# A fused attention and feed-forward kernel on one core: its head recut by deadline, later operands put in order two pairs ahead

**Chip, cores, metric.** One core of one Trainium2 chip. The time is device microseconds of one execution, in float32 input and output; lower is better. Executions of one kernel mostly agree within one or two per cent. A run more than 1.5% above the fastest of its kernel is classed "slow" and left out of every ratio here; the medians and ranges in the tables are of all runs.

## The reference

Eight batches, eight heads, 576 tokens and 16 "beacon" tokens of 64 columns. Attention with a causal mask (beacons are always seen), then two matrix products with a leaky ReLU between them. Cut to what matters:

```python
k_all = concatenate([beacon_k, k], axis=2); v_all = concatenate([beacon_v, v], axis=2)
scores = matmul(q, k_all^T) / sqrt(64)           # [8, 8, 576, 592]
scores = where(causal, -1e9, scores)             # the 16 beacon columns are never masked
a = exp(scores - max); a /= a.sum(-1) + 1e-9
x = matmul(a, v_all)  -> [4608, 512]             # heads side by side
h = x @ w_in                                     # w_in  [512, 2048]
out = maximum(0.01 * h, h) @ w_out               # w_out [2048, 512]
```

## The kernel before

Two heads are handled at once, a **pair**; there are 32 pairs, four to a batch. Per pair: scores on TensorE in four tiles, exp on ScalarE, causal masks on GpSimd, the product with the values (augmented by a column of ones for the row sums), a division on VectorE, and a transpose into `xT`. The feed-forward is cut into **fills**: four matmuls of 128x512 of it, 0.865 us, which TensorE runs between the attention's steps. Fills need all four pairs of a batch and the weights, so nothing is there to fill with before pair 6. The **head** is everything up to the last transposes of pair 7.

In the first eight pairs TensorE itself transposes q and k. Later pairs come through a DMA transpose, and GpSimd copies each pair's operands into order just before they are needed. The loads of q, k and the weights are issued from GpSimd's queue, in its program order, and cast to bfloat16 under way (those of the first pair, and here those of the beacons' keys, go through SyncE's and ScalarE's queues as float32); the values come through SyncE's queue as float32 and are cast by GpSimd.

The parts that the change touches, cut:

```python
    def load_v(b, after=None):
        # ... six loads on SyncE's queue into v_raws[b]; with `after`, the first waits for that load
    def cast_v(b, eng, c0=0, c1=NKB):                 # v_raw (float32) -> v_aug (bf16), by row tiles
    def in_order(g):                                  # GpSimd: beacon columns, qT, kT of a later pair
    def masks(g):                                     # GpSimd: four affine_selects on aT
    # ...
    with order:
        first = load_first_pair()
        make_identity(nc, ident)
        load_qk(0, 0); load_qk(0, 1)
        load_beacon_k(1, B, nc.sync)
        load_v(0, after=first)
        load_v(1)                                     # right behind batch 0's values
        # ...
        cast_v(0, nc.gpsimd, 0, 1)
        load_qk(1, 0)
        cast_v(0, nc.gpsimd, 1, 3)
        warm_up(34)                                   # unused matmuls
        beacon_transposes(0, 1); t_q(0, 0); t_q(0, 1, nc.scalar.copy)

        def loads(g):                                 # what is issued at the start of pair g
            if g == 1:   cast_v(0, nc.gpsimd, 3, 5)
            elif g == 2: load_qk(1, 1)
            elif g == 3: cast_v(1, nc.gpsimd, 0, 3); load_w_in(0)
            elif g == 4: cast_v(1, nc.gpsimd, 3, 5); load_w_in(1); load_w_in(2)
            # ...
            elif g >= 8: in_order(g + 1)              # one pair ahead
        for g in range(NG + 3):
            if g < 8:
                score(g, 0); score(g, 1)
                finish(g - 3)
                if g == 2: beacon_transposes(1, B)    # all later batches at once
                t_q(g + 1, 0); t_q(g + 1, 1)
                if g > 2: value(g - 2, 0)
                # ... a fill at g == 7
                score(g, 2); score(g, 3)
                # ...
                value(g - 2, 1)
                masks(g)
```

The softmax here doesn't subtract the row's maximum and nothing guards it: scores larger than these inputs give would overflow.

## Time and profile before

| | before |
|---|---|
| time, median of the first 3 runs | 356.92 us (356.29 to 357.59) |
| span of the profiled run | 354.4 us |
| TensorE busy | 340.3 us, 96% |
| its idle time | 14.1 us, of which 7.7 in the first 50 us |

A line of stretches gives the stretch in us, its length, the busy time (and instructions) of PE (TensorE), PEld (its weight loads), DVE (VectorE), ACT (ScalarE) and POOL (GpSimd), then the granted TensorE clock, the mean busy share of the DMA engines (it can read above 1; here it serves to compare), and GB/s moved. Two stretches of the kernel before that the result will be held against:

```profile
14.00:22.00 8.00, 7.35 (x111) 4.89 (x107) 5.36 (x12) 5.57 (x8) 7.92 (x18) 0.55 1.14 204
...
30.00:36.00 6.00, 5.62 (x148) 4.25 (x147) 4.81 (x13) 5.53 (x8) 6.00 (x12) 1.00 1.10 175
```

The transfers are at full rate from 14 to 22 us, and TensorE is busy from 30 to 36 us. In the table in order of time, a line gives start, length, engine, line, operation, and in brackets what ended the idle time before it.

```profile
14.14 0.68 SPq L210 DMA_DIRECT2D v_raw<-in_beacon_v_dram  x1
```

### The profile page before, as it was taken

To read this page: it belongs to the slowest core of one execution; us is meant where nothing else is said; L and a number is where in the kernel's file an instruction comes from. 1 tells how busy PE (TensorE), PEld (TensorE's weight loads), DVE (VectorE), ACT (ScalarE), POOL (GpSimd) and SP (SyncE) were. 2 spreads that over 40 slices of the span, in tenths; PEclk is the share of its full clock that TensorE was granted. 3 is DMA by queue.
4 is the path that set the end of the run, shared out by engine and by line. 5 is a ranking of instruction groups with operands and counts; after the bars stand their busy time and mean duration, and the time that the engine had idled before them with its cause. 6 is when DMAs were issued, how large, how long until landed. Compare 5 with 4: busy or idle time off the path is not lost.

```text
span 354.4 us, 7340 instructions
## 1 busy us (share of the span) xinstructions
PE 340.3 (96%) x3002; PEld 172.2 (49%) x3002; DVE 93.9 (27%) x231; ACT 189.3 (53%) x278; POOL 202.0 (57%) x343
## 2 busy tenths in 40 slices
PE   5889999999899999999999999999999999999996
PEld 4466554444454454444444444444444554444444
DVE  2387430102243223212222223222322241000111
ACT  3869754576445873478337843685358303633300
POOL 7699927499899899967695769574431100000000
PEclk9589999999999999999999999999999999999999
DMA  8999999998696976992589356900110011000012
GB/s 169 211 211 156 190 203 193 227 214 121 160 197 117 176 139 126 129 230 43 96 171 207 51 98 115 176 2 1 61 59 2 1 61 59 2 30 30 31 60 88
DMA packets 86929, 40.87 MB, mean 115 GB/s; under 512 B 69872, under 2 KB 82160, under 8 KB 86896
## 3 DMA queue, kind: packets, MB, share of 16 engines
q1 hardware_dynamic: 73456, 26.75, 35.1%
q0 software_dynamic: 13152, 13.34, 24.9%
q8 instruction: 23, 0.38, 0.4%
q10 hardware_dynamic: 288, 0.33, 0.4%
q14 instruction: 10, 0.08, 0.1%
HBM read 37.22 MB, written 9.44 MB: 132 GB/s over the span
## 4 chain that ended last, share of the span: by engine, by line
PE 72%; POOL 12%; DMA 10%; issue 2%; DVE 2%; SPq 1%; ACT 0%; POOLq 0%
PE acc L409 32%; PE acc L387 27%; PE av L351 6%; PE sc L297 6%; DMA w_out_sb<-in_moe_w_out_dram 4%; POOL aT L320 4%; DMA v_raw<-in_v_dram 3%; DMA q_raw<-in_q_dram 2%; POOL v_aug L224 2%; DMA v_raw<-in_k_dram 1%; PE tp L373 1%; POOL qT L277 1%; POOL q_raw L135 1%; DVE osb L418 1%; POOL kT L277 1%
## 5 line engine op out<-in xcount | busy, mean ns | idle before, releaser
L387 PE MATMUL acc<-xT,w_in_sb 128*128 128x512 bf16 x576 | 140.2, 379 | 1.4 <-DVE xT L378 1.4
L409 PE MATMUL acc<-w_out_sb,gT 128*128 128x512 bf16 (+1 forms) x592 | 139.6, 373 | 0.0
L306 ACT ACTIVATE aT<-sc 128x1024 bf16<-128x1024 f32 (+3 forms) x128 | 104.4, 869 | 64.1 <-PE sc L297 63.8
L394 ACT ACTIVATE gT<-acc 128x512 bf16<-128x512 f32 x144 | 85.9, 601 | 79.2 <-PE acc L387 79.2
L409 PEld LDWEIGHTS <-gT 128*128 128x128 bf16 x592 | 53.3, 98 | 58.7 <-issue 6.1
L320 POOL TENSOR_SCALAR_AFFINE_SELECT aT<-aT 128x384 bf16<-128x384 bf16 (+2 forms) x128 | 52.5, 449 | 50.2 <-PE av L351 40.3
L387 PEld LDWEIGHTS <-w_in_sb 128*128 128x128 bf16 x576 | 51.9, 98 | 59.5 <-issue 4.2
L418 DVE COPY osb<-acc 128x512 f32<-128x512 f32 (+1 forms) x37 | 25.1, 677 | 134.7 <-PE acc L409 134.6
L351 PEld LDWEIGHTS <-aT 128*128 128x128 bf16 (+1 forms) x960 | 37.5, 99 | 14.7 <-issue 2.6
L297 PE MATMUL sc<-qT,kT 64*128 64x80 bf16 (+4 forms) x384 | 37.0, 296 | 4.9 <-ACT aT L306 1.6
L351 PE MATMUL av<-v_aug,aT 128*128 128x65 bf16 (+1 forms) x960 | 40.7, 196 | 0.0
L361 DVE TENSOR_TENSOR x_nat<-av,rec 128x384 bf16<-128x384 f32 x64 | 31.4, 491 | 2.2
L224 POOL CAST v_aug<-v_raw 128x512 bf16<-128x512 f32 (+1 forms) x40 | 23.3, 619 | 8.9 <-DMA v_raw<-in_v_dram 8.8
L277 POOL COPY qT<-q_turn 128x576 bf16<-128x576 bf16 x24 | 28.1, 1171 | 0.0
L277 POOL COPY kT<-k_turn 128x576 bf16<-128x576 bf16 x24 | 28.0, 1167 | 0.0
L378 DVE COPY xT<-tp 128x576 bf16<-128x576 bf16 x32 | 14.5, 454 | 49.5 <-PE tp L373 49.5
L297 PEld LDWEIGHTS <-kT 64*128 64x128 bf16 x384 | 12.8, 96 | 30.4 <-issue 17.6
L360 DVE RECIPROCAL rec<-av 128x6 f32<-128x6 f32 x64 | 11.9, 187 | 58.9 <-PE av L351 58.9
L135 POOL DMA_DIRECT2D k_raw<-in_k_dram x31 | 19.3, 623 | 4.6 <-DMA w_out_sb<-in_moe_w_out_dram 4.5
L135 POOL DMA_DIRECT2D q_raw<-in_q_dram x31 | 19.0, 613 | 3.0 <-DMA w_out_sb<-in_moe_w_out_dram 2.8
L164 POOL COPY q_nat<-q_raw 128x1152 bf16<-128x1152 bf16 x12 | 13.7, 1146 | 5.5 <-DMA q_raw<-in_q_dram 5.5
L373 PEld LDWEIGHTS <-x_nat 128*128 128x128 bf16 (+2 forms) x160 | 11.1, 97 | 9.3 <-DVE x_nat L361 1.9
(36 smaller groups left out, 85.4 us busy)
## 6 DMA issues: line engine op xcount, KB each, us to landing
out_dram<-osb SPq DMA_DIRECT2D x35, 256.0 KB, 2.2
v_raw<-in_v_dram SPq DMA_DIRECT2D x24, 256.0 KB, 5.2
q_raw<-in_q_dram POOLq DMA_DIRECT2D x31, 144.0 KB, 5.1
k_raw<-in_k_dram POOLq DMA_DIRECT2D x31, 144.0 KB, 5.3
w_in_sb<-in_moe_w_in_dram POOLq DMA_DIRECT2D x4, 512.0 KB, 7.0
w_out_sb<-in_moe_w_out_dram POOLq DMA_DIRECT2D x4, 512.0 KB, 13.3
v_raw<-in_v_dram SPq DMA_DIRECT2D x8, 224.0 KB, 3.8
v_raw<-in_v_dram SPq DMA_DIRECT2D x8, 160.0 KB, 5.1
```

Source lines behind the costliest of these rows:

```text
L135: dma = nc.gpsimd.dma_start(out=dst[e * RP : (e + 1) * RP], in_=src[b, h0 : h0 + 2].rearrange("h (p i) d -> p h i d", i=RI),)
L224: eng.tensor_copy(out=dst[0 : ROWS[c], c, :, 0:D], in_=t[0 : ROWS[c], c])
L277: nc.gpsimd.tensor_copy(out=dst.rearrange("c (p i) -> c p i", i=RI), in_=t[:, :, e].rearrange("c i p -> c p i"),)
L297: nc.tensor.matmul(out=sc[:, par, col - c0 : col - c0 + w], lhsT=kT[ps_, c * 128 : (c + 1) * 128], rhs=qT[ps_, q0 : q0 + w], start=True, s ...
L306: nc.scalar.activation(out=aT[:, :, c0 : c0 + w], in_=sc[:, :, 0:w], func=AF.Exp, scale=0.125)
L320: nc.gpsimd.affine_select(out=part, in_=part, compare_op=ALU.is_ge, fill=0.0, base=base, channel_multiplier=-1, pattern=pattern,)
L351: nc.tensor.matmul(out=avv[:, n, 0 : D + 1], lhsT=aT[0 : ROWS[c], par, a0 : a0 + 128], rhs=va[0 : ROWS[c], c, 2 * hp + par, :], start=(c = ...
L361: nc.vector.tensor_tensor(out=x_nat[:, t0:t1].rearrange("p t e d -> p (t e) d"), in0=avv[:, :, 0:D], in1=rec[:, n0:n1, None].to_broadcast( ...
L387: nc.tensor.matmul(out=acc, lhsT=w_in_sb[:, j, fc * 128 : (fc + 1) * 128], rhs=xT[:, j, i * 512 : (i + 1) * 512], start=(j == 0), stop=(j ...
L394: nc.scalar.activation(out=gT[i][:, fc, :], in_=acc, func=AF.Prelu, alpha=0.01)
L409: nc.tensor.matmul(out=acc[:, 0:w], lhsT=gT[i][:, fc, t * 128 : (t + 1) * 128], rhs=w_out_sb[:, fc, c0 : c0 + w], start=(fc == 0), stop=(f ...
L418: nc.vector.tensor_copy(out=osb[:, 0:w], in_=acc[:, 0:w])
```

## The change

The intent is to load each thing by its deadline and to keep the clock up. In five parts:

1. **First pair**: the first k cast is halved between ScalarE and VectorE, and the first copy into kT is cut in two pieces, both on ScalarE; beacons of batches 0 and 1 only are prepared at first.
2. **Clock**: unused matmuls (`keep_busy`) fill TensorE's waits before the first scores and between the score tiles of pairs 0 and 1; VectorE does the masks of these two pairs.
3. **The gate**: batch 1's values wait until the last load of q and k for pairs 4 and 5 has landed. `w_in` comes in two loads and not four.
4. **Beacons** of batches 2 to 7 are transposed late, between fill 20 and fill 21 ahead of pair 8.
5. **Order**: later operands are put in order two pairs ahead, in GpSimd's queue ahead of the masks, with a third `kT` buffer.

The diff, cut to its core:

```diff
-    k_bufs = [... for i in range(2)]
+    k_bufs = [... for i in range(3)]
-    def load_w_in(i):        # quarters
+    def load_w_in(half):     # halves; w_out too
...
-        load_beacon_k(1, B, nc.sync)
         load_v(0, after=first)
-        load_v(1)
...
+        keep_busy(24)
+        beacon_transposes(0, 2)
...
+        nc.scalar.copy(out=first_cast[1][:, 0], in_=first_raw[1][:, 0])
+        nc.vector.tensor_copy(out=first_cast[1][:, 1], in_=first_raw[1][:, 1])
+        keep_busy(18)
+        t_q(0, 0)
+        keep_busy(4)
+        t_q(0, 1, nc.scalar.copy)
+        keep_busy(3)
...
+        cast_v(0, nc.gpsimd, 0, 2)
+        load_qk(1, 0, (0,))
         def loads(g):
             if g == 1:
-                cast_v(0, nc.gpsimd, 3, 5)
+                cast_v(0, nc.gpsimd, 2, 5)
+                load_v(1, after=load_qk(1, 0, (1,)))      # the gate
...
+            elif g == 4:
+                load_qk(1, 1, (1,))
+                load_w_in(0)
+                cast_v(1, nc.gpsimd, 0, 3)
+            elif g == 5:
+                load_w_in(1)
+                cast_v(1, nc.gpsimd, 3, 5)
+                load_w_out(0)
...
             elif g >= 2 * NPAIR:
-                in_order(g + 1)
...                                      # pairs 0 to 7
+                    if g in (1, 2):
+                        masks_by_tri(g - 1)               # on VectorE
+                if g < 2:
+                    keep_busy(3)                          # 7 and 4 further on
...                                      # ahead of pair 8
-                for n in range(22):
+                for n in range(20):
                     fill()
+                beacon_transposes(2, B)
+                fill()
+                fill()
+                in_order(g)
+                in_order(g + 1)
...                                      # pairs from 8 on, behind their last scores
+                if has(g + 2):
+                    in_order(g + 2)
```

## The prediction

> **What bounds the kernel now.** I read the page's table of slices first. TensorE is full but for the first tenth of the span.
>
> ```profile
> PE   5889999999899999999999999999999999999996
> ...
> PEclk9589999999999999999999999999999999999999
> ```
>
> The reader is to see two gaps in one place: slices 1 to 3 are below 9 and the granted clock falls to half in slice 2. The page gives PE 340.3 us busy of a span of 354.4, so 14.1 us idle. The table of stretches splits this.
>
> ```profile
> 0.00:5.00 5.00, 3.39 (x35) 3.22 (x35) 0.45 (x8) 1.58 (x2) 4.19 (x12) 1.00 0.57 135
> 5.00:8.00 3.00, 0.99 (x36) 0.75 (x36) 1.89 (x5) 1.32 (x2) 1.36 (x4) 0.92 1.23 214
> 8.00:21.00 13.00, 11.29 (x181) 7.31 (x181) 6.41 (x13) 10.26 (x13) 9.31 (x19) 0.50 1.20 217
> 21.00:36.00 15.00, 13.21 (x320) 9.27 (x318) 12.06 (x31) 12.91 (x17) 14.99 (x30) 0.99 1.08 173
> 36.00:50.00 14.00, 13.43 (x177) 8.14 (x176) 6.47 (x19) 8.82 (x14) 8.88 (x18) 1.00 1.21 194
> ```
>
> The columns are the stretch, its length, then PE, PEld, DVE, ACT, POOL busy, clock, DMA share and GB/s. From 8 to 21 us the clock is 0.50, and DMA is saturated up to 60 us at about 200 GB/s. Next, TensorE's waits:
>
> ```profile
> PE sc L297 <- ACT aT L306: 1.6, 4, 0.7
> PE sc L297 <- POOL kT L277: 1.5, 2, 1.1
> PE av L444 <- POOL ident masks.py:199: 1.4, 1, 1.4
> PE acc L387 <- DVE xT L378: 1.4, 6, 0.2
> PE tp L247 <- DVE q_cast L471: 1.0, 1, 1.0
> PE tp L247 <- ACT k_cast L472: 0.9, 1, 0.9
> ```
>
> All but the second and fourth lie in the first 50 us; the second is at 88.4 and 96.3 us, when scores wait for GpSimd to put operands in order. So the kernel is bound by TensorE work, plus a head that is not, plus one small GpSimd stretch. Idle after 100 us is 1.5 us between matmuls and a tail of 3 us for the last output; nothing of that is touched.
>
> **What the Trainium skill says.** "TensorE: Matmul & The Clock Gate", Part 1, states that the array falls to half clock after an idle window of about 3.4 us and returns after a busy one. The trace agrees: after a dense run to 4.8 us come 2.9 us with 1.0 us of matmuls, then the clock is 0.50, until dense work from 18.0 to 21.2 us brings back 1.00. "DMA: Bandwidth & Descriptors", Queues, rings and completion order, says each DMA engine takes turns between the queue rows that have work; so later loads slow those needed sooner. The trace shows the first v tile landing only at 12.3 us though issued at 6.4. "SBUF — State Buffer", Who interferes with whom, says a VectorE instruction with two SBUF inputs contends with GpSimd reads; the new mask multiplies are such, and this trace shows none.
>
> **The change part by part.**
>
> *Head's first pair.* The first k cast, 1.15 us on ScalarE, is split between two engines (about 0.6 us), and the first kT copy (0.64) in two. The second k half lands at 6.05 as before, so transposes run at about 6.7, and the first exp starts at some 8.25 instead of 9.17. Gain 0.9.
>
> *Clock.* Unused matmuls (24+18+4+3 before, 14 in each of pairs 0 and 1) fill TensorE's waits. At 98 ns each (34 took 3.34 us) 14 are 1.4 us of a pair of 3.3 us, where ScalarE sets the pace, so they cost nothing there. If the clock stays full, the work of 8.5 to 21 us shrinks. Cold and warm per pair: first two score tiles 0.92 and 0.51, both transposes 1.10 and 0.69, last two score tiles 0.83 and 0.41, values of a pair 1.76 and 1.14. Three pairs of scores and transposes, one of values, and the seven beacon transposes make 11.3 against some 6.5: 5 us less TensorE work, but not 5 us less time, because ScalarE now limits. Its exps:
>
> ```profile
> 28.27 3.26 ACT L306 ACTIVATE aT<-sc 128x832 bf16<-128x832 f32 x4 [0.17 <-PE sc L297]
> 32.00 3.26 ACT L306 ACTIVATE aT<-sc 128x832 bf16<-128x832 f32 x4 [0.47 <-PE sc L297]
> ```
>
> Eight pairs at 3.26 from 8.25 end at 34.3; before, the last exp ended at 41.5. Before had done three fills (units of feed-forward, 0.865 us) by then, after one, so 7.1 − 1.7 = **5.4 us** is the ideal gain of the head. This includes the 0.57 us wait for x_nat at 42.2, since a fill now stands ahead of that transpose.
>
> *Against it, DVE.* Per pair it has two copies of 0.76, reciprocals 0.20 + 0.18, products 0.56 + 0.42, xT 0.46: 3.33 us, just over ScalarE's 3.26. The kT copies that ScalarE took in two pairs return to it, and the masks of two pairs (1,152 columns each) cost it about 1 us a pair (my estimate from the 0.46 us of a 576-column bf16 copy). Loss about **0.4**.
>
> *Against it, DMA.* Batch 1's values now wait until its first keys have landed, about 20 us. From 20 us, 1.2 MB of values, 0.59 MB of q and k and half of w_in (1.05 MB) at 200 GB/s end at 34.2, while the fill in pair 7 would want w_in at about 32.5. Meanwhile GpSimd stands at the casts of those values, ahead of its masks. Some of that hides; I put **1.0**.
>
> *Against it, beacon transposes of batches 2 to 7.* They leave pair 2 for a place two fills ahead of the scores of pair 8, and the operands of pair 8 now begin with their result. Chain: transposes 0.4 with 0.2 of latency, two DVE copies 0.7, then on GpSimd:
>
> ```profile
> 59.90 0.20 POOL L275 COPY kT<-bkT 128x16 bf16<-128x16 bf16 x1
> ...
> 60.04 1.17 POOL L277 COPY qT<-q_turn 128x576 bf16<-128x576 bf16 x1
> ...
> 61.15 1.17 POOL L277 COPY kT<-k_turn 128x576 bf16<-128x576 bf16 x1
> ```
>
> That is 2.4 us, in all 3.8 from the transposes to the scores, against 0.4 + 2 × 0.865 = 2.1 of TensorE work in between: a new wait of **1.7**. Before, these operands were ready at 62.3 and used at 68.1.
>
> *Operands two pairs ahead.* They take the 1.5 us of waits on kT away; but GpSimd needs 7.2 us a pair there (order 2.5, masks 1.6, and per pair permutes 1.15, casts 0.7, issues 1.2), and TensorE only 6.3 to 7.9, so I leave 0.3. Gain **1.2**. Masks come 2.4 us later, with more than a pair of slack.
>
> Sum: −5.4 + 0.4 + 1.0 + 1.7 − 1.2 = −3.5, so 356.9 − 3.5 = **353.4 us**.
>
> **Rivals.**
>
> *The clock falls all the same.* For it: during 8.5 to 18 us TensorE was over 80% busy and yet stayed at 0.50, so a few gaps hold it there. Against: dense work now reaches from 1.4 to 7.7 us with no long gap, and between 21 and 36 us the clock held although idle pieces of 0.7 us occur. If it falls, some 3 us of the gain goes: 356 to 357.
>
> *The transfers become the bound.* DMA moves about 10.7 MB before the operands of pair 8, and before took until 57.7 us. A hole between about 15.5 and 20 us, opened by the gate, cannot be made up at 200 GB/s. If w_in lands 3 us late and GpSimd's queue holds the masks too, TensorE loses 2 to 3 us more: 355 to 356.
>
> *All goes smoothly.* The loads arrive in order, the beacon wait is hidden by TensorE being late anyway, and both gains count: −5.4 − 1.5 gives 350.0. This is the floor that I see, and 2% would need 349.8.
>
> *The gain is only moved.* The head was never on the path, GpSimd and DMA set the time at 96 us. The chain of waits before does run through q_raw's load (7.3 us) and GpSimd to pair 12. Then the head's gain is worth only what the loads get earlier, perhaps 2 us: 355.
>
> **Range and chances.** The floor of 350 and the bad cases of 356 frame it; I take 350.4 to 356.6. Faster by over 2% needs all gains and no new wait: 0.07. Slower would need the clock lost and both stalls: 0.02. Within 2%: 0.91.
>
> **What would show it.** Right: clock 1.00 through 8 to 21 us; the first exp near 8.3 and the last near 35 to 36; exps of pairs 0 to 6 back to back; pair 8's first scores waiting 1 to 2 us for kT behind the beacon copies; no long wait at 88 and 96. Wrong: a clock of 0.50 with the unused matmuls in place; TensorE waiting over 2 us on w_in or v_aug; scores of pairs 10 to 12 waiting on GpSimd as before; mask multiplies well over 1 us a pair. The prediction fails if the loads, whose landing I estimated from a mean rate, come several us earlier or later.

## More of the kernel before

```profile
24.65 1.74 POOL L224 CAST v_aug<-v_raw 128x512 bf16<-128x512 f32 x3
26.32 0.77 POOL L109 DMA_DIRECT2D w_in_sb<-in_moe_w_in_dram  x1
...
28.64 1.20 POOL L224 CAST v_aug<-v_raw 128x512 bf16<-128x512 f32 x2
```

Batch 1's values begin to be issued at 14.14 us. GpSimd casts them at 24.65 and 28.64 us, and neither line has a bracket: the data were there before GpSimd came to them.

## The result

| | before | after |
|---|---|---|
| median | 356.72 us (4 runs, 356.29 to 357.59) | 359.47 us (4 runs, 358.80 to 366.08, the last one slow) |
| ratio of fast runs | 1 | 1.0068, 95% interval 1.0039 to 1.0097 |
| span of the profiled fast run | 354.4 us | 357.5 us |

A ratio is the mean time of one kernel's fast runs over that of the other's of the same rounds, so it isn't quite the ratio of the medians. By the 2% rule the two are the same, as the prediction gave 0.91 for. But the time lies 2.9 us above the top of its range, and the interval says slower. (2% of this time is 7.1 us, so the class holds even though a gain was forecast and a loss came.)

Line numbers moved: the cast is now L227, scores L306, exps L315, masks on GpSimd L355, values L386, the ordering copies L286. The table of slices of the kernel after, answering to the prediction's first fence:

```profile
PE   8995799989999999999999999999999999999996
...
PEclk9999699999999999999999999999999999999999
```

The clock gap of slice 2 is gone. A new one is in slice 5, and TensorE has 5 and 7 tenths in slices 4 and 5. The stretches of the kernel after:

```profile
8.00:14.00 6.00, 5.50 (x118) 3.46 (x116) 2.64 (x4) 5.82 (x9) 0.82 (x2) 1.00 1.17 221
14.00:22.00 8.00, 7.17 (x173) 5.03 (x172) 7.05 (x19) 7.29 (x10) 7.95 (x18) 1.00 0.70 103
...
30.00:36.00 6.00, 1.97 (x41) 1.31 (x42) 2.03 (x4) 2.49 (x4) 3.10 (x7) 0.88 1.14 213
36.00:50.00 14.00, 11.61 (x157) 7.70 (x160) 5.93 (x18) 6.24 (x9) 11.98 (x23) 0.81 1.16 192
```

From 8 to 22 us the head runs as it was meant to, at full clock. But the transfers drop to 103 GB/s from 14 to 22 us, where before had 204. (GB/s counts bytes as written, and a load that casts float32 to bfloat16 writes half of what it reads. The busy share of the DMA engines, 0.70 against 1.14, is the fairer measure: the hole is some four tenths deep.) From 30 to 36 us TensorE works 1.97 us of 6.00, and after that the clock is down again. TensorE's waits in the kernel after:

```profile
PE av L386 <- POOL v_aug L227: 4.1, 1, 4.1
PE av L386 <- POOL aT L355: 1.7, 3, 1.2
PE sc L306 <- POOL kT L286: 1.5, 1, 1.5
```

The first two are new and lie in the head. The third is pair 8 waiting behind the late beacons; the two waits on `kT` at pairs 11 and 12 are gone. SyncE's queue and GpSimd in order of time, after:

```profile
21.36 0.33 SPq L213 DMA_DIRECT2D v_raw<-in_beacon_v_dram  x1
```

```profile
24.73 0.80 POOL L110 DMA_DIRECT2D w_in_sb<-in_moe_w_in_dram  x1
26.71 0.62 POOL L227 CAST v_aug<-v_raw 128x512 bf16<-128x512 f32 x1 [1.18 <-DMA v_raw<-in_v_dram]
...
30.85 0.62 POOL L227 CAST v_aug<-v_raw 128x512 bf16<-128x512 f32 x1 [2.24 <-DMA v_raw<-in_v_dram]
...
37.18 1.17 POOL L227 CAST v_aug<-v_raw 128x512 bf16<-128x512 f32 x2 [3.23 <-DMA v_raw<-in_v_dram]
```

The values are issued 7.2 us later than before, and now GpSimd stands at every cast for its data. Half of `w_in` was issued at 24.73, between the pieces of the values, and shares the transfers with them. What TensorE sees:

```profile
37.85 1.05 PE L386 MATMUL av<-v_aug,aT 128*128 128x65 bf16 x15 [4.06 <-POOL v_aug L227]
...
72.48 0.59 PE L306 MATMUL sc<-qT,kT 64*128 64x512 bf16 x4 [1.53 <-POOL kT L286]
```

The values of pair 4 stop for 4.06 us. When they go on, 15 matmuls take 1.05 us: the idle piece has cost the clock as well (0.50 from 36 to 40 us).

**Where the time went.** TensorE's program order fixes how many fills lie ahead of a point, so a point's start can be compared when one fill counts 0.865 us. The last transposes of the head begin at 48.73 us before, with 8 fills done, and at 51.20 after, with 7. Corrected to 8 fills, after is 3.3 us behind there. At the scores of pair 8 it is 72.48 + 0.865 against 68.08, 5.3 behind: the late beacons cost 2.0. At pair 13 (106.53 against 103.00) it is 3.5 behind, since before had its 1.5 us of waits between. The span ends 3.1 behind. So in this profile the head alone carries the loss, and the rest sums to about zero.

### The profile page after: what moved, and what is told of

The parts are those of the page before. It is cut to its first block, busy times and chain, and to the rows that moved or that the text cites.

```text
span 357.5 us, 7350 instructions
## 1 busy us (share of the span) xinstructions
PE 338.9 (95%) x3001; PEld 174.2 (49%) x3045; DVE 95.7 (27%) x235; ACT 187.6 (52%) x277; POOL 198.4 (55%) x340
## 4 chain that ended last, share of the span: by engine, by line
PE 77%; DMA 13%; issue 4%; POOL 2%; DVE 2%; SPq 1%; ACT 0%; POOLq 0%; ACTq 0%
PE acc L444 33%; PE acc L422 29%; PE av L386 6%; PE sc L306 6%; DMA v_raw<-in_v_dram 5%; DMA w_out_sb<-in_moe_w_out_dram 4%; DMA q_raw<-in_q_dram 2%; DMA v_raw<-in_k_dram 1%; PE tp L408 1%; DMA k_raw<-in_k_dram 1%; DVE osb L453 1%; DVE xT L413 1%; POOL v_aug L227 1%; SPq L218 1%; POOL aT L355 0%
## 5 line engine op out<-in xcount | busy, mean ns | idle before, releaser
L422 PE MATMUL acc<-xT,w_in_sb 128*128 128x512 bf16 x552 | 138.2, 380 | 3.0 <-DVE xT L413 1.4
L315 ACT ACTIVATE aT<-sc 128x1024 bf16<-128x1024 f32 (+3 forms) x128 | 103.9, 869 | 69.3 <-PE sc L306 66.7
L444 PE MATMUL acc<-w_out_sb,gT 128*128 128x512 bf16 (+1 forms) x572 | 136.6, 373 | 1.5 <-issue 0.8
L355 POOL TENSOR_SCALAR_AFFINE_SELECT aT<-aT 128x224 bf16<-128x224 bf16 (+1 forms) x120 | 48.4, 444 | 14.7 <-PE av L386 9.9
L386 PEld LDWEIGHTS <-aT 128*128 128x128 bf16 (+1 forms) x960 | 37.4, 98 | 21.2 <-issue 5.4
L386 PE MATMUL av<-v_aug,aT 128*128 128x65 bf16 (+1 forms) x960 | 41.1, 195 | 5.9 <-POOL v_aug L227 4.1
L286 POOL COPY qT<-q_turn 128x576 bf16<-128x576 bf16 x24 | 28.5, 1186 | 29.4 <-PE sc L306 15.0
L306 PE MATMUL sc<-qT,kT 64*128 64x80 bf16 (+4 forms) x384 | 36.1, 285 | 3.0 <-POOL kT L286 1.5
L227 POOL CAST v_aug<-v_raw 128x512 bf16<-128x512 f32 (+1 forms) x40 | 23.1, 617 | 13.8 <-DMA v_raw<-in_v_dram 13.8
L286 POOL COPY kT<-k_turn 128x576 bf16<-128x576 bf16 x24 | 28.5, 1186 | 0.0
L306 PEld LDWEIGHTS <-kT 64*128 64x128 bf16 x384 | 12.5, 94 | 27.9 <-issue 14.3
## 6 DMA issues: line engine op xcount, KB each, us to landing
w_in_sb<-in_moe_w_in_dram POOLq DMA_DIRECT2D x2, 1024.0 KB, 10.7
```

The source lines that it names most:

```text
L227: eng.tensor_copy(out=dst[0 : ROWS[c], c, :, 0:D], in_=t[0 : ROWS[c], c])
L286: nc.gpsimd.tensor_copy(out=dst.rearrange("c (p i) -> c p i", i=RI), in_=t[:, :, e].rearrange("c i p -> c p i"),)
L306: nc.tensor.matmul(out=sc[:, par, col - c0 : col - c0 + w], lhsT=kT[ps_, c * 128 : (c + 1) * 128], rhs=qT[ps_, q0 : q0 + w], start=True, s ...
L315: nc.scalar.activation(out=aT[:, :, c0 : c0 + w], in_=sc[:, :, 0:w], func=AF.Exp, scale=0.125)
L355: nc.gpsimd.affine_select(out=part, in_=part, compare_op=ALU.is_ge, fill=0.0, base=base, channel_multiplier=-1, pattern=pattern,)
L386: nc.tensor.matmul(out=avv[:, n, 0 : D + 1], lhsT=aT[0 : ROWS[c], par, a0 : a0 + 128], rhs=va[0 : ROWS[c], c, 2 * hp + par, :], start=(c = ...
```

## The experiments

The theory that I formed from this: the gate opens a hole in the transfers that later loads can't make up, and the stall at the values, with the clock lost behind it, is what failed. A first rival: the late beacons set the time. A second: what one transfer gives up, another takes, so that the head's gain can't be had anyway. (Where an expectation below uses letters or names of theories, they are that expectation's own.)

All times, medians in us, with the kernel before on the same chip:

| run | kernel | median (range) | before | ratio of fast runs, 95% |
|---|---|---|---|---|
| a1_ungated | after, no gate | 353.82 (352.44 to 355.29) | 356.96 | 0.9914, 0.9863 to 0.9965 |
| a2_beacon_early | after, beacons earlier | 359.55 (357.27 to 362.77) | 356.96 | 1.0053, 0.9988 to 1.0117 |
| a3_both | both | 355.21 (351.63 to 357.81) | 356.96 | 0.9904, 0.9816 to 0.9992 |
| b1_order_ahead | before, part 5 alone | 355.20 (354.46 to 357.25) | 356.96 | 0.9961, 0.9907 to 1.0015 |
| b2_gate | before, gate alone | 359.12 (358.59 to 361.44) | 357.06 | 1.0073, 1.0022 to 1.0123 |
| c1_early_qk | both, q and k earlier | 354.90 (354.05 to 356.66) | 357.06 | 0.9948, 0.9900 to 0.9996 |
| d1_no_busy | no gate, no unused matmuls in pairs 0, 1 | 354.12 (352.90 to 356.64) | 357.06 | 0.9929, 0.9874 to 0.9985 |
| e1_w_late | after, `w_in` behind the casts | 359.80 (358.72 to 360.28) | 357.06 | 1.0084, 1.0036 to 1.0131 |
| f1_quarters | both, `w_in` in four | 353.92 (352.43 to 356.99) | 356.35 | 0.9938, 0.9896 to 0.9980 |
| a3_again | both | 354.44 (353.65 to 355.09) | 356.35 | 0.9945, 0.9916 to 0.9974 |
| a1_again | no gate | 355.51 (354.66 to 357.25) | 356.35 | 0.9977, 0.9942 to 1.0013 |
| g1_half_gate | after, gate one load earlier | 360.02 (354.05 to 360.88) | 356.35 | 0.9957, 0.9905 to 1.0010 (2 runs) |
| after_again | after | 360.76 (358.51 to 364.20) | 356.65 | 1.0094, 1.0065 to 1.0124 |
| a3_third | both | 356.83 (352.96 to 358.60) | 356.65 | 0.9974, 0.9931 to 1.0017 |
| i1_no_v1 | both, batch 1's values not loaded (wrong) | 355.21 (352.40 to 357.79) | 356.65 | 0.9935, 0.9902 to 0.9968 |
| j1_qk_earlier | f1, later q and k issued earlier | 353.87 (352.55 to 354.89) | 356.84 | 0.9919, 0.9889 to 0.9949 |
| f1_again | f1 | 353.49 (351.51 to 359.41) | 356.84 | 0.9881, 0.9847 to 0.9915 |

Where TensorE stands in some profiles, one for each run, against before, by the reckoning above (minus is earlier):

| profile | head's last transposes begin, fills done | head | pair 8 | end of span |
|---|---|---|---|---|
| before | 48.73, 8 | 0 | 0 | 0 |
| after | 51.20, 7 | +3.3 | +5.3 | +3.1 |
| a1_ungated | 45.58, 7 | -2.3 | -0.3 | -2.5 |
| after_again | 52.72, 7 | +4.9 | +6.8 | +4.6 |
| a1_again | 47.35, 7 | -0.5 | +1.4 | -0.3 |
| a3_both | 48.37, 7 | +0.5 | +0.8 | -1.0 |
| a3_third | 46.66, 7 | -1.2 | -0.9 | -3.0 |
| b1_order_ahead | 51.61, 8 | +2.9 | +2.9 | +1.1 |
| b2_gate | 51.05, 8 | +2.3 | +2.3 | +3.1 |
| e1_w_late | 50.71, 7 | +2.8 | +4.8 | +2.6 |
| a3_again | 46.14, 7 | -1.7 | -1.4 | -1.5 |
| i1_no_v1 | 44.56, 7 | -3.3 | -3.0 | -0.1 |

The head of one kernel scatters: by 1.6 us between the two profiles of the kernel after, and by 2.8 us among the five without the gate. b1_order_ahead has no gate, and its profile, of the slowest of its runs (357.25), still stands at +2.9 here.

### The gate

**Taken away** (a1_ungated):

```diff
-                load_v(1, after=load_qk(1, 0, (1,)))
+                load_qk(1, 0, (1,))
+                load_v(1)
```

> The changed kernel, with the values of batch 1 loaded without waiting for the keys of batch 1. Theory (the gate starves the head): the 4.1 us wait of the value matmuls for v_aug, the 1.7 us for masks behind the casts, and the half clock from 35 to 41 us all go; 4.5 to 6 us less than the changed kernel, so 353.5 to 355. Rival (the DMA engines are full, so bytes only change places): batch 1's q and k come later instead, the transposes of pairs 4 to 7 wait some 4 us more on them, and the time stays within 1 us of 359.3.

Measured: 0.9914, against 1.0068 and 1.0094 with the gate. A repeat on another chip (a1_again, below) gave 0.9977. The stretch, the first waits and GpSimd's casts of this run:

```profile
14.00:22.00 8.00, 5.56 (x147) 3.85 (x145) 5.57 (x15) 5.68 (x9) 7.19 (x17) 1.00 1.16 197
```

```profile
PE tp L253 <- DMA k_raw<-in_k_dram: 2.1, 2, 1.8
PE sc L306 <- POOL kT L286: 1.5, 1, 1.5
```

```profile
26.64 1.75 POOL L227 CAST v_aug<-v_raw 128x512 bf16<-128x512 f32 x3
...
30.78 1.18 POOL L227 CAST v_aug<-v_raw 128x512 bf16<-128x512 f32 x2
```

The transfers stay at 197 GB/s, the casts wait for nothing, and the waits on `v_aug` and on masks are gone. In their place k is 2.1 us late: what the gate was meant to prevent. In the two profiles the head is 5.6 us better without the gate (+3.3 against -2.3). Over the fast profiles of these two heads it is +3.3 and +4.9 with the gate and -2.3 to +0.5 without it, so the size is uncertain (2.8 to 7.2 us) and the direction is not.

**Put alone into the kernel before** (b2_gate): batch 1's values wait for the last of `load_qk(1, 0)`.

```diff
         load_v(0, after=first)
-        load_v(1)
...
-        load_qk(1, 0)
+        load_v(1, after=load_qk(1, 0))     # load_qk now returns its last load
```

> The kernel before, with the gate alone: values of batch 1 behind the last of q and k of batch 1's first two pairs. There w_in is issued behind the casts of these values, so nothing shares the transfers with them, and the head is some 4 us slower. Theory: they land by 28 us instead of 23, GpSimd stands 2 us at their casts and delays w_in and masks by that; 0 to 2 us longer, 357 to 359. Rival (the gate is harmful by itself): a wait for v_aug of 3 us or more, 360 and more.

Measured: 1.0073. The gate by itself costs as much as the whole change. The stretch, and GpSimd:

```profile
14.00:22.00 8.00, 7.20 (x100) 4.58 (x99) 5.10 (x12) 5.33 (x8) 7.25 (x16) 0.50 0.72 119
```

```profile
29.89 0.62 POOL L224 CAST v_aug<-v_raw 128x512 bf16<-128x512 f32 x1 [2.17 <-DMA v_raw<-in_v_dram]
30.45 0.77 POOL L109 DMA_DIRECT2D w_in_sb<-in_moe_w_in_dram  x1
```

The same hole (119 GB/s) and the same standing at the cast. `w_in`, behind the cast in GpSimd's queue, is issued at 30.45 and not 26.32. Here TensorE waited on masks (1.1 us) and ran at a lower clock (0.79 from 30 to 36 us), and the waits on `kT` at pairs 11 and 12 grew from 1.5 to 2.2. What shows the cost is the time: the head of this profile, +2.3, lies within the scatter of ungated ones (b1 has +2.9).

**`w_in` moved behind the first casts** (e1_w_late), to see whether the shared rate makes the stall:

```diff
-                load_w_in(0)
                 cast_v(1, nc.gpsimd, 0, 3)
+                load_w_in(0)
```

> The changed kernel, gate and all, with the first half of w_in issued behind the first three casts of batch 1's values instead of ahead of them. Theory A (the values come late because w_in takes half of the transfer rate from them): the last value tile lands near 30 instead of 37 us, the 4.1 us wait for v_aug falls under 1 us, but w_in lands at 36 or later and the first fill waits 2 to 4 us for it; time 357 to 359.5. Theory B (the late start at 21 us alone does it): the values land only 2 or 3 us earlier, the wait for v_aug stays above 2 us, and w_in adds its own, above 360.

Measured: 1.0084, no better. TensorE's waits:

```profile
PE acc L422 <- DMA w_in_sb<-in_moe_w_in_dram: 2.6, 1, 2.6
PE av L386 <- POOL aT L355: 2.5, 2, 2.3
PE sc L306 <- POOL kT L286: 1.5, 1, 1.5
```

The wait on `v_aug` fell from 4.1 to 0.2 us, and the last casts ran at 33.90 and not 37.18, so `w_in` did take the rate from the values. But 2.6 us of waiting for `w_in` and 2.5 for masks came instead. The bytes missing from the hole are missing somewhere; the order only picks who waits.

**Half a gate** (g1_half_gate): the values wait for the q and k of pair 4 alone, which land earlier.

```diff
-        load_qk(1, 0, (0,))
+        load_v(1, after=load_qk(1, 0, (0,)))
...
-                load_v(1, after=load_qk(1, 0, (1,)))
+                load_qk(1, 0, (1,))
```

> The changed kernel with the gate moved forward: values of batch 1 behind q and k of the first of the four head pairs' loads of batch 1 (landing at about 19.4) instead of the second (21.4). Theory (time lost is proportional to how long the transfers stand half empty): values start 2 us earlier, the hole shrinks from 8 to about 5 us, time between the gated 359.4 and the ungated 353.8, about 357. Rival (any gate is equally bad because w_in catches up with the values): 359, or (the gate's harm is only at the last tile) 354.

Measured: two runs of 354.05 and 355.65, and four of 359.89 to 360.88, classed slow. The profile is of a fast one (355.65): values issued from 17.75, 2.3 us of waiting on `v_aug`, 1.1 on k. Inconclusive in time: I can't say whether the four are the slow state or a second course of this kernel.

**The same chip for both** (after_again, a3_third): the kernel after unchanged, and after without the gate and with the earlier beacons.

> The changed kernel unedited, on the same chip as the two below. If the gate is the main cause, it stays 4 to 6 us above the ungated one with early beacon transposes, at 359 to 360; if the 6 us miss was chip to chip scatter, the two are within 2 us.

> Ungated and early beacon transposes, beside the changed kernel: 353.5 to 355.

Measured: 1.0094 and 0.9974 of the same runs of before, so the gate and the late beacons together cost 0.0120 of 356.65, some 4.3 us. a3_third itself, at 356.83, missed its forecast of 353.5 to 355. In this profile of the kernel after the stall shows as 5.4 us of waiting on masks and only 0.6 on `v_aug`: GpSimd stood 4.53 us at its last cast (35.64) with the masks behind it. The same cause with another name in the table of waits.

### The late beacons

**Earlier by six fills** (a2_beacon_early), and **together with no gate** (a3_both):

```diff
-                for n in range(20):
-                    fill()
-                beacon_transposes(2, B)
-                fill()
-                fill()
+                for n in range(22):
+                    if n == 14:
+                        beacon_transposes(2, B)
+                    fill()
```

> The changed kernel, with the beacon transposes of batches 2 to 7 put six fills earlier (after 14 of the 22 fills rather than after 20). Theory (the chain transposes, copies, order is the new wait at pair 8): the 1.5 us wait for kT at 72.5 us goes, 1.2 to 1.6 us less, about 357.9. Rival (GpSimd is short of time there anyway): the same 1.5 us come back at pairs 10 to 12 or as masks late, and the time stays at 359.3.

> Both edits together. If both theories hold and the waits are independent: 6 to 7.5 us less than the changed kernel, 352 to 353.5, so about 1% faster than the kernel before. If the loads bound the start of batch 2 (its q and k landing after 57 us whatever the head does), pair 8 waits on GpSimd again and the two edits give less than their sum, about 355.

Measured: a2 1.0053, a3 0.9904. In both the wait on `kT` at pair 8 is gone. a2's profile fell in a slow run (362.77) with 9.9 us of waiting on `v_aug`, so the gate's scatter hides what the beacons are worth in time. The late beacons as the whole cause fall: with the beacons mended and the gate left, the kernel is still no faster than before.

**Both again, on one chip** (a3_again, a1_again):

> The kernel ungated and with early beacon transposes once more, for a tighter interval. If the 1.5 us wait at pair 8 was on the path: 1 to 1.5 us below the ungated kernel run beside it. If it was slack that GpSimd's or the loads' lateness takes up: no difference.

> The ungated kernel once more, for a tighter interval: 353 to 354.5, ratio to before about 0.991, so 5 to 6 us below the changed kernel.

Measured: 354.44 with the earlier beacons, 355.51 without, which missed its forecast of 353 to 354.5; the intervals overlap, so by time this is likely but not shown. By the profiles it is clear: from the head's end to pair 8 the late beacons cost some 2.0 us in all five profiles of the table that have them late (after twice, a1_ungated, a1_again, e1_w_late), and 0.3 in the four that have them early. So 1.7 is what moving them costs. a3_again gave part of it back as 1.9 us of waits on `kT` at pairs 11 and 12.

### Operands two pairs ahead

**Part 5 alone on the kernel before** (b1_order_ahead). To make room for the third `kT`, the first casts go into tiles that are unused then, as in the kernel after.

```diff
-    k_bufs = [... for i in range(2)]
+    k_bufs = [... for i in range(3)]
...
-                if has(g + 1):
-                    in_order(g + 1)
...
                 in_order(g)
+                in_order(g + 1)
                 cast_v(2, nc.gpsimd)
...
                 score(g, 3)
+                if has(g + 2):
+                    in_order(g + 2)
```

> The kernel before with one part of the change alone: three kT buffers, operands put in order two pairs ahead and ahead of the masks. Theory: the waits of 0.4 and 1.1 us for kT at pairs 11 and 12 go, 1.2 to 1.5 us less, about 355.4. Rival (GpSimd has too much to do from 64 to 96 us, so a lead of one pair only moves the wait to masks or to later pairs): no gain, 356.5 to 357.

Measured: 0.9961, which is 1.4 us, with an interval that just includes 1; the 1.5 us of waits at pairs 11 and 12 are gone from its table. The step holds in mechanism, and its size fits.

### The clock and the unused matmuls

**No unused matmuls between the score tiles** (d1_no_busy), on top of no gate:

```diff
-                if g < 2:
-                    keep_busy(3)        # and 7, and 4
```

> The ungated kernel without the 14 unused matmuls in each of pairs 0 and 1 (those ahead of pair 0 stay). Theory (they keep the clock up): the matmuls of pairs 1 to 3 take cold times, an x18 transpose group 0.69 instead of 0.47 us and the values of pair 0 1.8 instead of 1.1, and the time is 1.5 to 3 us longer than ungated, about 356. Rival (ScalarE sets the pace of pairs 0 to 2, or the clock stays up anyway because the head has fewer gaps): within 1 us of 353.8.

Measured: 0.9929, beside a1's 0.9914 on another chip. Two stretches of its profile:

```profile
8.00:14.00 6.00, 4.02 (x96) 2.40 (x96) 2.82 (x5) 5.81 (x9) 1.79 (x4) 0.97 1.24 222
14.00:22.00 8.00, 7.66 (x145) 5.36 (x145) 5.74 (x15) 6.17 (x9) 7.26 (x16) 0.59 1.09 196
```

Without them the clock does fall, to 0.59 from 14 to 22 us, where a1 has 1.00. Yet the other three runs (352.90 to 354.13) are as fast as a1. A reading that fits is that ScalarE sets the pace in those pairs, and a TensorE of half speed still nearly keeps it; no run tests that alone. The profiled run was the slowest (356.64) and waited 3.3 us for `w_in`, so the matmuls may be worth something on a bad run; the medians differ by 0.3 us, but both intervals reach some 0.5% (2 us) to either side. The unused matmuls ahead of pair 0 stayed, and the clock was 0.97 from 8 to 14 us, so what the clock is worth there is not tested.

### Where the rest of the head's gain goes

Without the gate the head is 2.3 us better than before in a1's profile, and less in the others, and not 4.0. Five runs look for the rest.

**q and k of pair 4 issued ahead of the casts of batch 0's values** (c1_early_qk):

```diff
-        cast_v(0, nc.gpsimd, 0, 2)
         load_qk(1, 0, (0,))
+        cast_v(0, nc.gpsimd, 0, 2)
```

> Both edits of the former run, and q and k of batch 1's first pair issued ahead of the casts of batch 0's values instead of behind two of them (about 7 us rather than 14 us). Theory (in the ungated kernel the head still stalls on late issue of these loads, 1.6 to 3.2 us): the waits of the transposes of pair 4 on q_raw and k_raw go, no drop of the clock at 20 us, 350.5 to 352.5. Rival (DMA bytes only change places): batch 0's values come later instead, the value matmuls of pair 0 wait 1 to 2 us for v_aug at 17 us, and the time is as without the edit, 353 to 354.

Measured: 0.9948, no better than a3. The waits on q and k are gone; waits of 1.0 and 0.5 us on batch 0's `v_aug` came in their place at 17 to 19 us, and the clock fell with them (0.79 from 14 to 22 us). That fits the second rival: at some 200 GB/s the bytes only change places.

**Batch 1's values not loaded at all** (i1_no_v1); the casts read batch 0's, and the result is wrong (relative error 0.41).

```diff
                 load_qk(1, 0, (1,))
-                load_v(1)
+                v_raws[1] = v_raws[0]
```

> Ungated, early beacon transposes, and the values of batch 1 not loaded at all: the casts read batch 0's values a second time. The result is wrong on purpose; all instructions but six loads (1.2 MB) stay. Theory (the loads bound the head): the waits on q_raw, k_raw and w_in go, exps of the eight pairs stand back to back, the clock holds, 351 to 352.5, near the 350 that I saw as the floor. Rival (ScalarE, VectorE and GpSimd bound the head as well): within 1 us of the kernel with the loads, 353.5 to 354.5.

Measured: 0.9935. The head ran freely: first score tiles of pairs 3 to 7 at 17.79, 21.29, 24.78, 28.34 and 31.90, 3.5 us apart, pair 7 5.3 us ahead of before. Then 2.2 us were lost waiting for `w_in`, which leaves -3.3 at the head's end, and would be -5.5 without that wait:

```profile
PE acc L422 <- DMA w_in_sb<-in_moe_w_in_dram: 2.2, 1, 2.2
```

The transfers are no fuller here from 14 to 22 us (106 GB/s) than behind the gate: with the values not needed, the hole does no harm. At pair 8 3.0 us are still there. At the end of this run (355.98; the median is 355.21) 0.1 is. GpSimd and TensorE in it:

```profile
90.07 1.14 POOL L167 COPY q_nat<-q_raw 128x1152 bf16<-128x1152 bf16 x1 [3.73 <-DMA q_raw<-in_q_dram]
```

```profile
94.67 0.77 PE L306 MATMUL sc<-qT,kT 64*128 64x512 bf16 x4 [2.25 <-POOL kT L286]
95.38 1.89 PE L444 MATMUL acc<-w_out_sb,gT 128*128 128x512 bf16 x4
```

TensorE came to pair 12 so early that GpSimd was still standing at a load of q for batch 3 (3.73 us), and pair 12's `kT` was behind it. The wait was 2.25 us, with 0.65 at pair 11. Then the clock was down: a fill of 1.89 us where 1.03 is usual. So the whole lead went: 1.4 us of waiting more than before has, and by estimate some 1.5 us by the clock, since pairs 12 and 13 are 8.27 us apart here and 6.73 before.

**`w_in` in four loads** (f1_quarters, f1_again), and **later q and k issued a place earlier** on top of it (j1_qk_earlier):

```diff
     def load_w_in(half):
-        cols = slice(half * DF // 2, (half + 1) * DF // 2)
+        for i in (2 * half, 2 * half + 1):          # one load each
+            cols = slice(i * 512, (i + 1) * 512)
```

> Ungated, beacon transposes early, and w_in in four loads as before instead of two. Theory (the last stall of the head is the first fill waiting for half of w_in, 0.7 us in two profiles and 3.3 in another): it needs a quarter only, that wait goes, mean 0.5 to 1.5 us below the same kernel with halves, about 353. Rival (one stall of the head only uncovers the next, since the transfers are booked out): same as with halves within 0.5 us.

Measured: 0.9938, no wait on `w_in` and none on `kT`, 2.1 us on k. It can't be told from a3_again (0.9945, same chip).

```diff
             if has(g):
                 masks(g)
+                if g % NPAIR == 0 and g // NPAIR < B - 1:
+                    load_qk(g // NPAIR + 1, 1)      # was issued a pair later
```

> Ungated, beacon transposes early, w_in in four loads, and q and k of the second half of each next batch issued one pair earlier (behind the masks of the batch's first pair). Theory (what the head gains is lost again at pairs 11 and 12, where GpSimd stands 2 to 4 us at q_raw and orders kT late): GpSimd's waits on q_raw from 76 to 110 us go, kT is never waited for there, 0.5 to 1.5 us below the kernel beside it, about 352.5 to 353.5. Rival (GpSimd's own work or the head's scatter decides): no difference.

> The kernel that the former is one edit away from, on the same chip: 353.5 to 355.

Measured: j1 0.9919 and f1 0.9881, same chip. In j1's trace GpSimd doesn't stand at q from 76 to 110 us, and no wait on `kT` is left. f1's profile here fell in the slow state (359.41) and has that wait (2.6). So j1 does what it should, but f1's fast runs (351.51 to 354.15) don't need it. What j1 may give is steadiness: its six runs lie within 2.3 us, none slow, where f1 had two slow ones. Six runs don't settle that.

**The version to keep** is f1 or j1: 0.6 to 1.2% under before (three measurements) and, through before, 1.3 to 2.1% under after, by dividing their ratios by 1.0068 and 1.0094 (different chips, so rough).

## Why the prediction was wrong

The predicted class (within 2%) was right; the number and the range were not: 353.4 was given, 350.4 to 356.6, and 359.47 came. By its own steps:

- **Head's first pair: right.** The first exp was at 8.76 us in this profile, against 8.25 predicted and 9.17 before. There k's data came to the cast only at 6.50 us. In after_again, with k cast at 6.13, the exp was at 8.26, and in the other kernels with this head at 8.00 to 8.67.
- **Clock: right, but worth little.** It was 1.00 from 8 to 22 us, as said. In d1 it was lost from 14 to 22 us, and the median was 0.3 us from a1's, on another chip, so no gain of this step shows there; from 8 to 14 us it was not tested.
- **5.4 us ideal gain of the head: about right.** With no values to load the head was 5.5 us ahead, its wait on `w_in` set aside, where the step and VectorE's 0.4 together make 5.0. It is one profile, and of no kernel with correct results.
- **"Against it, DVE": right in what was measured.** The mask multiplies took 1.03 and 0.95 us a pair, about 1 predicted; the loss of 0.4 was not measured apart. Of the contention with GpSimd of which the page "SBUF — State Buffer" of the Trainium skill (Who interferes with whom) warned, the profile shows no sign: a GpSimd cast that overlaps the first multiplies took 0.62 us, as elsewhere. But the two hardly overlap, so it is not tested.
- **"Against it, DMA ... I put 1.0": this is the step that failed.** The head came out at +3.3 and not at the -4.0 of this sum, so this term, taken as all that the other steps leave, was 8.3 and not 1.0: 5.6 by the gate (head of after against a1_ungated) and 2.7 that the ungated kernel pays too, most of it waiting 2.1 us on k. Each is from one profile: over the others the gate's part is 2.8 to 7.2 and the ungated kernel's 2.7 to 5.5. In the times of one chip the gate and the late beacons make some 4.3 us. The step added up bytes from 20 us to the last byte of `w_in`, and held that against the fill that needs `w_in`. The first to run dry was another: the values matmuls of pair 4, which need all five tiles of `v_aug`. Three things were missed. The hole was 8 us long, with the DMA engines at six tenths of what before had (busy share 0.70 against 1.14 from 14 to 22 us), and not 4.5 us. `w_in`, issued at 24.73, shares the rate with the values and so delays what was needed sooner, as the Trainium skill, "DMA: Bandwidth & Descriptors", Queues, rings and completion order, would have it and the prediction itself quoted; e1_w_late agrees, where the last casts ran 3.3 us earlier without it. And a stall of 4 us takes the clock with it, so that it costs more than its length.
- **"Against it, beacon transposes ... 1.7": right.** The wait was 1.5 us, and moving the transposes measured 1.7.
- **"Operands two pairs ahead", gain 1.2: right.** 1.5 us of waits went; alone it gave 1.4, with an interval that just includes 0.
- **The rivals.** "The transfers become the bound" had the mechanism, the hole, GpSimd's queue and the masks behind it, but named `w_in` as what comes late and stopped at 356. "The gain is only moved" came true for the part of the head's gain that i1 uncovered: it was lost again at pair 12.

With 8.3 in place of the 1.0 the prediction's sum, -5.4 + 0.4 + 8.3 + 1.7 - 1.2, is +3.8, against +3.5 at pair 13 and +3.1 at the end of the spans. (The 8.3 was taken from the head of this same profile, so this checks only the last two terms.)

On the spread of the ungated kernels, 351.5 to 359.4: two fast profiles with the same program up to the head's end differ by 2.8 us there, a3_both (+0.5) and a1_ungated (-2.3). In a3_both TensorE waited 3.2 us for q and k at 20 to 22 us, GpSimd behind it stood 3.37 us ahead of masks (25.74), so `w_in` was issued at 28.27 and not 25.88, and the transfers fell to 69 GB/s from 26 to 30 us, where a1_ungated has 141. So a late q or k seems to open a hole of its own through GpSimd's queue; two profiles don't show that it makes the whole spread.

Open: what else makes that spread; what g1's group at 360 is; what the earlier beacons are worth in time, beyond the profiles.

## What to carry to other kernels

Work out a gate on a load from the first consumer that runs dry, not from the last byte: list what each engine needs next, when, and how many bytes stand ahead of it, the loads it will share the rate with included. Where transfers were the limit here, a gap in them was not made up, and reorderings (e1, c1) only chose who waits; look for it as a fall of GB/s and of the DMA engines' busy share in the stretch ahead of the stall. An engine freed in one stage soon reaches the next stage's loads, so a gain there must be followed to the end of the program before it is counted.

## What the Trainium skill lacked or had wrong

- "TensorE: Matmul & The Clock Gate", HAM oscillation, gives as a rule no idle gaps above some 3.4 us. A shorter one was enough here: in i1_no_v1 a gap of 2.25 us was followed by a fill of 1.89 us (1.03 warm) and a clock of 0.50 from 96 to 98 us. A gap of the same 2.25 us, at 99.93 in f1_again (a slow run), left it at 1.00. Nor does the page say how dense "busy" must be: the clock stayed at 0.50 with TensorE busy 4.95 of 6.00 us (before, 8 to 14 us), and at 0.97 with 4.02 of 6.00 (d1_no_busy, same stretch). Its warning that clock events in traces can't always be trusted agrees: b1_order_ahead reads 1.00 from 8 to 14 us, but its first score tiles there took 0.99 us by its trace, where warm ones took 0.59:

```profile
8.81 0.99 PE L302 MATMUL sc<-qT,kT 64*128 64x512 bf16 x4 [0.74 <-ACT kT L255]
```

- "DMA: Bandwidth & Descriptors", Anatomy of one DMA, fits a load issued from GpSimd by 2.0 us plus bytes over 436 GB/s, an estimate of 4.4 us for half of `w_in` (1,024 KB as written), or 6.8 if its float32 bytes as read are counted. In the kernel after those two loads took 10.7 us to land, beside others. The page has no figure for loads that cast, nor for what loads in flight together get of the rate beyond the taking of turns.
- No page has the cost of a load that makes GpSimd's queue stand at a cast with masks and further loads behind it: 4.53 us in after_again, and 5.4 us of TensorE waiting on masks.
